# S4 convolution and gated FFN in one kernel: zero products moved behind the last z products, an `rs` operation and two groups of sums moved, z rooms filled by channel block

## The chip, the cores and the metric

The kernel runs on one core of a Trainium2 chip as one launch. The metric is device time in microseconds (us); the runs of a kernel are summed up by their median. The core's engines are PE (TensorE: matmuls, with PEld for the weight loads that overlap them), DVE (VectorE), ACT (ScalarE), POOL (GpSimd) and SP (SyncE, which only issues DMAs here). ACT and POOL issue DMAs too. Each engine works through its own instructions in order and waits by semaphores for the others.

## What is computed

The reference is an adaLN block on 2048 tokens of 640 channels, in float32. Cut to what matters:

```
h = layernorm(x) * (1 + ca) + sa
x = x + ga * s4(h)            # long convolution by FFT, plus u * Dskip
h = layernorm(x) * (1 + cb) + sb
gate, up = h @ w1, h @ w3     # 640 x 1728 each
x = x + gb * ((silu(gate) * up) @ w2)
```

`s4` builds a kernel of length 2048 for each channel from 128 complex modes and convolves it with `h`; the reference does it by FFT of twice the length.

## The kernel before

**First part, 0 to about 368 us.** The convolution is done as a two-step transform of 32 x 64 points, channel block by channel block (5 blocks of 128 channels). The result before its last step, called z, goes to a scratch in DRAM (`zs`) as it comes. The last step multiplies z by a constant matrix `i2` on PE.

**Second part, the output phase.** The tokens are 16 tiles of 128, in four quarters of four tiles; two quarters (A and B) make a pair. For each x tile, `x_get` (L1150 to 1162) loads the tile of x and its z rows, `x_mid` (L1164 to 1177) multiplies z by `i2` into PSUM, adds the result to x on DVE and takes the layer norm's statistics, `x_norm` normalises on ACT, and `x_turn` transposes four tiles at a time on PE into the operands `xA0` to `xA4` and `xB0` to `xB4`. The FFN has 14 blocks of 128 hidden channels, named f = 0 to 13; the last one is half as wide and has gate and up in one tile. All its matmuls are done in a split form: each operand is a high and a low part (`gh` and `gl` for the gate weights, `uh` and `ul` for the up weights, made by an ACT cast and a DVE subtraction), and each product is three matmuls. Blocks f = 0, 13, 1 and 2 of the first pair are done plainly (`plain`, L1280), quarter A first, then quarter B in the order 2, 1, 13, 0; the others go through `seven` (L1338), which does two quarters with seven block products in place of eight and needs sums of operands (`x_sums`, L1219, split by `x_sum_split`, L1229).

**The transition.** The tiles of quarter A are prepared in the first part, all but the last channel block, whose products (`late_products`, L811, into the bank `pls`) come last. `x_stats` (L832 to 845) adds them to x, takes statistics and aggregates them (BN_AGGR, one for each of four tiles) on DVE, has POOL compute the power -1/2 of the variance, and DVE form `rs[:, 2]`, the negative mean times that. Only ACT's normalisation reads `rs[:, 2]`; ACT normalises tiles 0 and 2, DVE tiles 1 and 3. `x_first` (L1138) begins with `keep_warm(18)`, 18 matmuls of zeros by zeros, 128 x 128 by 128 x 512, into a bank of the pool `psA`. Then come the 20 transposes. The tiles of quarter B (4 to 7) are prepared while PE works on f = 0, 13 and 1 of quarter A: `beside` (L1563) issues one of the steps in the list `side` (L1560) behind each group of products.

**The preparation of pair 1.** While PE does the `w2` products of pair 0 (`outputs`, L1398, 28 steps of 15 or 10 products), the function `prepare` (L1486) puts one step of preparing eight x tiles beside each step. Six of them have no room of their own for z: `homes` (L1497) lists two operand tiles of pair 0 for each, which are no longer read. z of an x tile is 128 partitions (64 frequencies for either part of the channel blocks: blocks 0 and 1 in partitions 0 to 63, blocks 2 to 4 in 64 to 127) by 4 row groups by 3 blocks of 128. With homes, each of the two tiles holds two of the four row groups, and `z_load` (L847) fills it with five DMAs of 64 x 2 x 128. SP issues all of these, in order with the loads of x and of `xs`. ACT issues the loads of `w2` (`load(n + 4, S)`, L1436) between its casts. `x_mid` does 8 products for each tile: four row groups by two halves, with 256 or 384 columns. A matmul in float32 is two instructions in the trace.

**What sets the order.** A scheduler orders the instructions by their place in the code, as resources come free; where `in_order` is set, and where `tc.keep_in_program_order` or `tc.issue_after` ask for it, the order written in the code holds. The two pools' banks and the number of buffers of each name make an instruction wait for the last reader of what it overwrites. Nearly all operations are issued through one helper, so the profile shows them under its line, L114, and tiles are told apart by name.

Of the kernel before, what the change touches and what calls it, by code (L numbers as in the profile page):

```python
# [17 lines left out]
P = 128  # L18
# [15 lines left out]
NG = NA // 8  # L34
NPG = NPH + NG - 1
LATE = 5
TURN = 4294967296.0
EPS = 1e-5

# [80 lines left out]
def tile_kernel(ctx: ExitStack, tc: tile.TileContext, a):  # L120
# [655 lines left out]
    def zj(k, j):  # L776
        return zs[k, j % 4, j // 4].rearrange("l c f d -> (c f) l d")
# [54 lines left out]
    def x_stats():  # L832

        mv = xp.tile([P, 4, 2], F32, name="mv4", bufs=1)
        rs = xp.tile([P, 3, 4], F32, name="rs4", bufs=1)
        for j, (x, z, st) in enumerate(early):
            V.tensor_tensor(x[:, 512:], pls[j][:, :P], x[:, 512:], op=OP.add)
            V.bn_stats(st[:, 4, :], x[:, 512:])
            V.bn_aggr(mv[:, j, :], st)
        e = lambda i: epst[:, i:i + 1].broadcast_to([P, 4])  # L840
        G.tensor_tensor(rs[:, 0, :], mv[:, :, 1], e(0), op=OP.add)
        power = G.tensor_tensor(rs[:, 1, :], rs[:, 0, :], e(1), op=OP.pow)
        V.scalar_tensor_tensor(rs[:, 2, :], mv[:, :, 0], -1.0, rs[:, 1, :], op0=OP.mult, op1=OP.mult)
        moments.extend((mv, rs))
        return power

    def z_load(z, j, ks, q=nc.sync, b0=0):  # L847

        nb = z.shape[1]
        for k in ks:  # L850
            hh = int(k > 1)
            kk = k - 2 * hh
            ins = q.dma_start(z[hh * 64:hh * 64 + 64, :, kk * DC:kk * DC + DC], zj(k, j)[:, b0:b0 + nb])
        return ins

    def x_tile():
# [194 lines left out]
    for tk in range(NS + 1, LAG + 8 * NDC + 2):  # L1051
        do("st", tk)
        do("kc", tk)
        if tk == LAG + 8 * NDC:
            late_products(6)
        last = do("iv", tk - 1)
        do("zt", tk - 1)
        do("T", tk)
        do("Y", tk)
        if tk == NS + 1:  # L1060
            tabs.close()
            xp = ctx.enter_context(tc.tile_pool(name="xp", bufs=2))
            idle = xp.tile([P, 512], F32R, name="idle", bufs=1)
            G.memset(idle.bitcast(F32), 0.0)
            for j in range(4):
                early[j] = (x_tile(), early[j][1], xp.tile([P, KD, 6], F32, name="st5", bufs=4))
                G.memset(early[j][1][64:, :, 2 * DC:], 0.0)
            i2bt = [h_tile() for _ in range(8 - LATE)]
        i = tk - 1 - LAG - 8 * NDC + 8
        if 0 <= i < 8:  # L1070
            if i < 4:
                z_last_load = z_load(early[i][1], i, (3,), q=nc.gpsimd)
            if i == 3:
                with tc.issue_after(z_last_load.ins):
                    for t in range(8 - LATE):
                        for j in range(4):
                            nc.gpsimd.dma_start(i2bt[t][j * 32:j * 32 + 8], a["i2b"][:, t])
            for j in ((), (), (), (), (0,), (1,), (), (2, 3))[i]:
                x_part(j, last)
            if i == 6:  # L1080
                pl = psS.tile([P, 2, 512], F32, name="pl", tag="A", bufs=1)
                pls += [pl[:, 0], pl[:, 1]] + [psS.tile([P, 512], F32, name="pl", tag=t, bufs=1) for t in ("pk", "pb")]
                late_products(5)
            if i == 7:
                z_early()
                early_products()
                late_products(7)
    power = x_stats()
    for name in first_w:
        first_w[name] = xp.tile([P, KD, P], F32, name="rw", bufs=4)  # L1090
# [25 lines left out]

        return wq.tile([P, 512], F32, name=f"s{i}")

    IDLE = 18

    def keep_warm(n):

        ps = bank(0)
        for _ in range(n):
            tc.keep_in_program_order(PE.matmul(ps, idle[:, :P], idle, start=True, stop=True))

    def pair_tile(name, dt=F32R):

        return wq.tile([P, 2, 512], dt, name=name)
# [7 lines left out]

    def x_first(tiles):  # L1138

        keep_warm(IDLE)  # L1140
        mv, rs = moments
        for j, (x, z, st) in enumerate(early):
            xn = xn_tile(j)
            if j % 2 == 0:
                S.activation(xn, x, AF.Identity, scale=rs[:, 1, j:j + 1], bias=rs[:, 2, j:j + 1])
            else:
                V.tensor_scalar(xn, x, mv[:, j, 0:1], rs[:, 1, j:j + 1], op0=OP.subtract, op1=OP.mult)
            tiles.append(xn)

    def x_get(j, x, loaded=False, homes=None):  # L1150

        if homes:
            zs_ = [pair_tile(n, F32).rearrange("p a b -> p (a b)")[:, :768].rearrange("p (b d) -> p b d", b=2)
                   for n in homes]
        else:
            zs_ = [z_tile()]
        with tc.issue_after(zlast[0].ins):
            if not loaded:
                SQ.dma_start(x, a["x"][j * P:(j + 1) * P, :])
            for i, z in enumerate(zs_):  # L1160
                z_load(z, j, range(NDC), SQ, 2 * i)
        return [x, [zs_[b * len(zs_) // 4][:, b % (4 // len(zs_))] for b in range(4)]]

    def x_mid(j, got, g):  # L1164

        x, z = got
        py = [bank(g) for _ in range(2)]
        for b in range(4):
            for hh in range(2):
                r, c = slice(hh * 64, hh * 64 + 64), slice(b * NA, b * NA + NA)  # L1170
                n = ZW[hh]
                PE.matmul(py[hh][c, :n], i2[r], z[b][r, :n], start=True, stop=True, tile_position=(r.start, c.start))
        for hh in range(2):
            h = slice(hh * 256, hh * 256 + ZW[hh])
            V.tensor_tensor(x[:, h], py[hh][:, :ZW[hh]], x[:, h], op=OP.add)
        got.extend(ln_stats(xp, x))
        G.dma_start(xs[j], x)
# [6 lines left out]
        tiles.append(xn)  # L1184

    ends = [None, None]

    def x_split(name, xf):
        t = pair_tile(name)
# [48 lines left out]
    def split(src, shape, names, after=None, part=slice(None)):  # L1238
        hi = wq.tile(shape, F32R, name=names[0], bufs=2)
        lo = wq.tile(shape, F32R, name=names[1], bufs=2)  # L1240
        with ExitStack() as order:
            for ins in after or ():
                order.enter_context(tc.issue_after(ins.ins))
            S.copy(hi[:, part], src[:, part])
            V.tensor_tensor(lo[:, part], src[:, part], hi[:, part].bitcast(F32), op=OP.subtract)
        return hi, lo

    def weight(f, name, q=None):
# [281 lines left out]
    for pair in range(2):  # L1530
# [37 lines left out]
        for n, f in enumerate(simple):  # L1568
# [6 lines left out]
            if pair == 0 and n == 1:  # L1575
                with tc.issue_after(power.ins):
                    for j, (x, z, st) in enumerate(early):
                        G.dma_start(xs[j], x)

        for n, f in enumerate(simple[::-1]):  # L1580
            hB[f] = h_tile()
            ws = ws or plain_weights(f)
            plain("B", f, hB[f], ws)
            ws = None
            if pair == 0 and n < 2:
                x_sums(n)
                x_sum_split(n)
        for i in range(2):
            x_late(i)
        before = output  # L1590
# [77 lines left out]
```

## Time and profile before

| | us |
|---|---|
| runs of before | 938.29, 936.25, 935.79 |
| median | 936.25 |
| the profiled execution's own time | 939.53 |
| its span, first to last instruction | 937.6 |
| what lies around the span | 1.93 |
| mean granted TensorE clock | 0.970 of full |

The profile is of one execution of its own, which took 3.28 us longer than the median of the runs. Its page lists busy time by engine and by group of instructions; the trace behind it has each instruction's start and length, the idle time before it and what ended that. Busy shares in slices of the span run from 0 to 9 tenths:

```profile
PE   4888879999998898999999999899999999999997
PEclk9977789999999998999999999999999999999999
```

Each digit is a fortieth of the span, 23.4 us. The output phase begins in the sixteenth slice.

### The profile page before, as it was taken

Reading aid. Unit: us, or ns where it says so; the run is one execution under the profiler, and the core shown is the slowest. Engines: PE = TensorE matmul, PEld = TensorE weight load, DVE = VectorE, ACT = ScalarE, POOL = GpSimd, SP = SyncE. Lnnn points to the kernel's source line nnn. Section 1 sums busy time; section 2 is a strip of 40 time slices with the busy share of each in tenths; the row PEclk is TensorE's granted clock in tenths of the full one; section 3 lists DMA queues with packets and bytes.
Section 4 is the critical chain, followed back from the end, with each engine's and each line's share of the span. In section 5 each row is a group of like instructions: output and inputs, shape, how many; then the busy total and the mean of one; then the engine's idle time right before and its main releaser. Section 6 shows DMA issues by size and latency. Waiting matters only on the chain.

```text
span 937.6 us, 20100 instructions
## 1 busy us (share of the span) xinstructions
PE 875.5 (93%) x8036; PEld 668.3 (71%) x8036; DVE 700.2 (75%) x1209; ACT 541.3 (58%) x747; POOL 272.7 (29%) x285
## 2 busy tenths in 40 slices
PE   4888879999998898999999999899999999999997
PEld 2545456666666576788888886578888888888786
DVE  5899889999999967685666665677976666654684
ACT  6988889999999542474333332475633333323332
POOL 3333434553454221223222202210332222200341
PEclk9977789999999998999999999999999999999999
DMA  9664375676566968942121227946311322123352
GB/s 270 217 222 175 133 211 179 212 192 192 171 210 191 299 202 227 290 149 75 56 57 57 57 82 213 260 148 195 101 57 56 113 57 57 56 87 97 98 187 93
DMA packets 103808, 140.68 MB, mean 150 GB/s; under 512 B 20420, under 2 KB 62916, under 8 KB 103716
## 3 DMA queue, kind: packets, MB, share of 16 engines
q1 hardware_dynamic: 93012, 113.71, 40.2%
q10 hardware_dynamic: 8272, 18.16, 6.4%
q0 software_dynamic: 2432, 7.54, 2.5%
q8 instruction: 63, 1.03, 0.5%
q14 instruction: 29, 0.24, 0.1%
HBM read 107.92 MB, written 31.46 MB: 149 GB/s over the span
## 4 chain that ended last, share of the span: by engine, by line
PE 74%; ACT 9%; DVE 8%; issue 3%; SPq 3%; DMA 3%; DVEq 0%; ACTq 0%
PE ps L114 54%; PE p L114 7%; PE pz L114 4%; PE pt L114 3%; SPq L114 3%; PE pk L114 2%; PE pa L114 2%; ACT A L114 2%; ACT cs L114 1%; DVE uk L114 1%; DVE u L114 1%; ACT ph L114 1%; PE pu L114 1%; ACT uk L114 1%; ACT L114 1%
## 5 line engine op out<-in xcount | busy, mean ns | idle before, releaser
L114 DVE TENSOR_TENSOR s<-ps,s 128x512 f32<-128x512 f32 x138 | 94.9, 687 | 82.5 <-PE ps L114 82.2
L114 ACT CAST gh<-rw 128x640 fp32r<-128x640 f32 x87 | 63.3, 728 | 128.3 <-PE ps L114 86.4
L114 DVE TENSOR_TENSOR gl<-rw,gh 128x640 fp32r<-128x640 f32 x87 | 78.0, 896 | 69.0 <-ACT gh L114 68.6
L114 POOL TENSOR_TENSOR S<-rw 128x256 f32<-128x256 f32 x46 | 36.9, 805 | 234.9 <-DVE S0l L114 157.4
L114 PE MATMUL ps<-gh,uh 128*128 128x512 f32 x224 | 88.1, 393 | 0.0
L114 PE MATMUL ps<-gl,uh 128*128 128x512 f32 x224 | 87.7, 392 | 0.0
L114 PE MATMUL ps<-xA,gh 128*128 128x512 f32 x280 | 87.6, 391 | 0.0
L114 PE MATMUL p<-uk,s 128*64 128x256 f32 x576 | 71.6, 391 | 15.2 <-DVE Y L114 3.9
L114 POOL TENSOR_TENSOR ph<-thi,iota 128x1376 int32<-128x1376 int32 x20 | 51.2, 2562 | 117.8 <-DVE A L114 103.6
L114 DVE TENSOR_TENSOR E<-A,cs 128x1024 f32<-128x1024 f32 (+1 forms) x80 | 80.6, 1019 | 1.9 <-PE pk L114 1.3
L114 PE MATMUL ps<-gh,ul 128*128 128x512 f32 x208 | 81.6, 392 | 0.0
L114 ACT ACTIVATE A<-pa 128x1024 f32<-128x1024 f32 (+1 forms) x80 | 64.4, 815 | 10.2 <-PE pa L114 9.8
L114 PEld LDWEIGHTS p<-uk,s 128*64 128x64 f32 x576 | 41.3, 138 | 36.9 <-DVE Y L114 5.6
L114 PEld LDWEIGHTS ps<-xA,gh 128*128 128x128 f32 x280 | 52.3, 188 | 12.5 <-ACT xA L114 0.7
L114 DVE TENSOR_TENSOR A<-A,ph 128x1024 f32<-128x1024 f32 x40 | 54.1, 1357 | 0.8
L114 PE MATMUL ps<-xA,gl 128*128 128x512 f32 x140 | 54.5, 389 | 0.0
L114 PE MATMUL pt<-s,K 128*64 128x128 f32 x640 | 45.1, 284 | 6.1 <-ACT uk L114 5.9
L114 PEld LDWEIGHTS ps<-gl,uh 128*128 128x128 f32 x224 | 42.5, 190 | 9.1
L114 PEld LDWEIGHTS ps<-gh,uh 128*128 128x128 f32 x224 | 42.5, 190 | 9.0 <-DVE h L114 0.2
L114 ACT ACTIVATE s<-ps 128x512 f32<-128x512 f32 (+1 forms) x33 | 19.7, 597 | 45.8 <-PE ps L114 45.8
L114 POOL TENSOR_TENSOR rw<-rw,gbr 128x512 f32<-128x512 f32 x14 | 20.4, 1458 | 88.7 <-DMA rw<-in_w_dram 77.3
L114 PEld LDWEIGHTS pt<-s,K 128*64 128x64 f32 x640 | 35.6, 140 | 14.5 <-ACT uk L114 9.7
(224 smaller groups left out, 2227.2 us busy)
## 6 DMA issues: line engine op xcount, KB each, us to landing
rw<-in_w_dram ACTq DMA_DIRECT2D x44, 320.0 KB, 3.0
us<-u SPq DMA_DIRECT2D x16, 640.0 KB, 3.5
rw<-in_wg_dram SPq DMA_DIRECT2D x31, 320.0 KB, 3.0
s<-in_s_dram SPq DMA_DIRECT2D x36, 256.0 KB, 4.0
i<-in_i_dram SPq DMA_DIRECT2D x36, 256.0 KB, 4.7
rw<-in_wu_dram SPq DMA_DIRECT2D x28, 320.0 KB, 2.9
uk<-us SPq DMA_DIRECT2D x16, 512.0 KB, 5.6
zs<-zt SPq DMA_DIRECT2D x16, 512.0 KB, 4.7
```

Source lines behind the costliest of these rows:

```text
L114: ins = fn(*args, **kw)
```

## The change

Four places change.

1. The zero products move from the head of `x_first` to right behind `late_products(7)`, ahead of `x_stats`. They are 16 now, and they go into the PSUM bank with the tag "Z", which the first part used for z.
2. `rs[:, 2]` moves from `x_stats` to `x_first` and is issued behind the last subtraction of the weight split of f = 0 (`last_split`). That split waits for `last_sum`, which is now the last BN_AGGR.
3. `x_get` with homes puts two channel blocks of all four row groups into the first tile ("wide") and one into the second ("narrow"). z comes in five DMAs of 64 x 4 x 128 for each x tile in place of ten of 64 x 2 x 128, and `x_mid` does 12 products with 256, 256 and 128 columns in place of 8 with 256 and 384.
4. `x_sums(n)` and `x_sum_split(n)` of the first two plain blocks of quarter B are issued behind `ends[1]`, the last DVE operation of the last `x_turn`.

```diff
--- before.py
+++ after.py
@@ -34,6 +34,7 @@
 NG = NA // 8
 NPG = NPH + NG - 1
 LATE = 5
+IDLE = 16
 TURN = 4294967296.0
 EPS = 1e-5
 
@@ -836,21 +837,19 @@
         for j, (x, z, st) in enumerate(early):
             V.tensor_tensor(x[:, 512:], pls[j][:, :P], x[:, 512:], op=OP.add)
             V.bn_stats(st[:, 4, :], x[:, 512:])
-            V.bn_aggr(mv[:, j, :], st)
+            last_sum[0] = V.bn_aggr(mv[:, j, :], st)
         e = lambda i: epst[:, i:i + 1].broadcast_to([P, 4])
         G.tensor_tensor(rs[:, 0, :], mv[:, :, 1], e(0), op=OP.add)
         power = G.tensor_tensor(rs[:, 1, :], rs[:, 0, :], e(1), op=OP.pow)
-        V.scalar_tensor_tensor(rs[:, 2, :], mv[:, :, 0], -1.0, rs[:, 1, :], op0=OP.mult, op1=OP.mult)
         moments.extend((mv, rs))
         return power
 
-    def z_load(z, j, ks, q=nc.sync, b0=0):
-
-        nb = z.shape[1]
+    def z_load(z, j, ks, q=nc.sync):
+
         for k in ks:
             hh = int(k > 1)
             kk = k - 2 * hh
-            ins = q.dma_start(z[hh * 64:hh * 64 + 64, :, kk * DC:kk * DC + DC], zj(k, j)[:, b0:b0 + nb])
+            ins = q.dma_start(z[hh * 64:hh * 64 + 64, :, kk * DC:kk * DC + DC], zj(k, j))
         return ins
 
     def x_tile():
@@ -1085,6 +1084,9 @@
                 z_early()
                 early_products()
                 late_products(7)
+    ps = psS.tile([P, 2, 512], F32, name="ps", tag="Z", bufs=1)[:, 0]
+    for _ in range(IDLE):
+        tc.keep_in_program_order(PE.matmul(ps, idle[:, :P], idle, start=True, stop=True))
     power = x_stats()
     for name in first_w:
         first_w[name] = xp.tile([P, KD, P], F32, name="rw", bufs=4)
@@ -1116,14 +1118,6 @@
 
         return wq.tile([P, 512], F32, name=f"s{i}")
 
-    IDLE = 18
-
-    def keep_warm(n):
-
-        ps = bank(0)
-        for _ in range(n):
-            tc.keep_in_program_order(PE.matmul(ps, idle[:, :P], idle, start=True, stop=True))
-
     def pair_tile(name, dt=F32R):
 
         return wq.tile([P, 2, 512], dt, name=name)
@@ -1137,8 +1131,9 @@
 
     def x_first(tiles):
 
-        keep_warm(IDLE)
         mv, rs = moments
+        with tc.issue_after(last_split[0].ins):
+            V.scalar_tensor_tensor(rs[:, 2, :], mv[:, :, 0], -1.0, rs[:, 1, :], op0=OP.mult, op1=OP.mult)
         for j, (x, z, st) in enumerate(early):
             xn = xn_tile(j)
             if j % 2 == 0:
@@ -1150,16 +1145,22 @@
     def x_get(j, x, loaded=False, homes=None):
 
         if homes:
-            zs_ = [pair_tile(n, F32).rearrange("p a b -> p (a b)")[:, :768].rearrange("p (b d) -> p b d", b=2)
-                   for n in homes]
+            wide, narrow = (pair_tile(n, F32).rearrange("p a b -> p (a b)") for n in homes)
+            wide = wide.rearrange("p (k b d) -> p k b d", k=2, b=4)
+            z = [wide[:, 0], wide[:, 1], narrow[:, :4 * DC].rearrange("p (b d) -> p b d", b=4)]
+            use = [(0, 2 * DC, wide.rearrange("p k b d -> p b k d")), (2 * DC, 3 * DC, z[2])]
         else:
-            zs_ = [z_tile()]
+            t = z_tile()
+            z = [t[:, :, k * DC:k * DC + DC] for k in range(3)]
+            use = [(0, 3 * DC, t)]
         with tc.issue_after(zlast[0].ins):
             if not loaded:
                 SQ.dma_start(x, a["x"][j * P:(j + 1) * P, :])
-            for i, z in enumerate(zs_):
-                z_load(z, j, range(NDC), SQ, 2 * i)
-        return [x, [zs_[b * len(zs_) // 4][:, b % (4 // len(zs_))] for b in range(4)]]
+            for k in range(NDC):
+                hh = int(k > 1)
+                r = slice(hh * 64, hh * 64 + 64)
+                SQ.dma_start(z[k - 2 * hh][r], zj(k, j))
+        return [x, use]
 
     def x_mid(j, got, g):
 
@@ -1168,8 +1169,12 @@
         for b in range(4):
             for hh in range(2):
                 r, c = slice(hh * 64, hh * 64 + 64), slice(b * NA, b * NA + NA)
-                n = ZW[hh]
-                PE.matmul(py[hh][c, :n], i2[r], z[b][r, :n], start=True, stop=True, tile_position=(r.start, c.start))
+                for lo, hi, part in z:
+                    n = min(hi, ZW[hh]) - lo
+                    if n > 0:
+                        rhs = part[r, b] if len(part.shape) == 4 else part[r, b, :n]
+                        PE.matmul(py[hh][c, lo:lo + n], i2[r], rhs, start=True, stop=True,
+                                  tile_position=(r.start, c.start))
         for hh in range(2):
             h = slice(hh * 256, hh * 256 + ZW[hh])
             V.tensor_tensor(x[:, h], py[hh][:, :ZW[hh]], x[:, h], op=OP.add)
@@ -1184,6 +1189,7 @@
         tiles.append(xn)
 
     ends = [None, None]
+    last_split = [None]
 
     def x_split(name, xf):
         t = pair_tile(name)
@@ -1242,7 +1248,7 @@
             for ins in after or ():
                 order.enter_context(tc.issue_after(ins.ins))
             S.copy(hi[:, part], src[:, part])
-            V.tensor_tensor(lo[:, part], src[:, part], hi[:, part].bitcast(F32), op=OP.subtract)
+            last_split[0] = V.tensor_tensor(lo[:, part], src[:, part], hi[:, part].bitcast(F32), op=OP.subtract)
         return hi, lo
 
     def weight(f, name, q=None):
@@ -1577,14 +1583,16 @@
                     for j, (x, z, st) in enumerate(early):
                         G.dma_start(xs[j], x)
 
+        turned = ends[1]
         for n, f in enumerate(simple[::-1]):
             hB[f] = h_tile()
             ws = ws or plain_weights(f)
             plain("B", f, hB[f], ws)
             ws = None
             if pair == 0 and n < 2:
-                x_sums(n)
-                x_sum_split(n)
+                with tc.issue_after(turned.ins):
+                    x_sums(n)
+                    x_sum_split(n)
         for i in range(2):
             x_late(i)
         before = output
```

The order on the engines moves as follows. In the rows, a name with a number is one tile among several of its name, and x4 counts equal instructions in a row.

DVE, end of the first part, before: BN_AGGR is the aggregate, `gl` and `ul` are the low parts of f = 0's weights, the row with `rs_4831` on both sides is `rs[:, 2]`, and the TENSOR_SCALAR rows normalise tiles 1 and 3.

```order
L114 BN_STATS st_4431<-xm 128x6
L114 BN_AGGR mv_4830<-st_4428 128x2
L114 TENSOR_TENSOR gl<-rw,gh 128x640
L114 BN_AGGR mv_4830<-st_4431 128x2
L114 TENSOR_TENSOR ul<-rw,uh 128x640
L114 SCALAR_TENSOR_TENSOR rs_4831<-mv_4830,rs_4831 128x4
L114 TENSOR_SCALAR T_4897<-xm,mv_4830,rs_4831 128x640
L114 TENSOR_SCALAR T_4901<-xm,mv_4830,rs_4831 128x640
```

The same place now:

```order
L115 BN_STATS st_4431<-xm 128x6
L115 BN_AGGR mv_4847<-st_4428 128x2
L115 BN_AGGR mv_4847<-st_4431 128x2
L115 TENSOR_TENSOR gl<-rw,gh 128x640
L115 TENSOR_TENSOR ul<-rw,uh 128x640
L115 SCALAR_TENSOR_TENSOR rs_4848<-mv_4847,rs_4848 128x4
L115 TENSOR_SCALAR T_4895<-xm,mv_4847,rs_4848 128x640
L115 TENSOR_SCALAR T_4899<-xm,mv_4847,rs_4848 128x640
```

The fourth aggregate has moved in front of `gl`.

ACT, around the `s` of f = 0 (s_5020), before. The first `uh` is the up weight of f = 1 and the first `gh` its gate weight; the `s` of f = 13 has 64 rows, T_5046, T_5095 and T_5120 are the normalised tiles 4 to 6, s_5192 is the `s` of f = 1, and the `gh` behind the 64-row `s` is the gate weight of f = 2:

```order
L114 CAST uh<-rw 128x640
L114 ACT_TABLE_LOAD
L114 ACTIVATE s_5020<-ps 128x512
L114 CAST gh<-rw 128x640
L114 ACTIVATE T_5046<-xm,rs 128x640
L114 ACTIVATE s_5069<-ps 64x512
L114 CAST gh<-rw 128x640
L114 ACTIVATE T_5095<-xm,rs 128x640
L114 ACTIVATE T_5120<-T_4971,rs 128x640
L114 ACTIVATE s_5192<-ps 128x512
L114 CAST uh<-rw 128x640
```

The same place now (s_5018 for f = 0, T_5044, T_5093 and T_5118 for tiles 4 to 6, s_5190 for f = 1):

```order
L115 ACT_TABLE_LOAD
L115 ACTIVATE s_5018<-ps 128x512
L115 CAST gh<-rw 128x640
L115 CAST uh<-rw 128x640
L115 ACTIVATE s_5067<-ps 64x512
L115 ACTIVATE T_5044<-xm,rs 128x640
L115 ACTIVATE T_5093<-xm,rs 128x640
L115 ACTIVATE T_5118<-T_4969,rs 128x640
L115 ACTIVATE s_5190<-ps 128x512
L115 CAST gh<-rw 128x640
L115 CAST uh<-rw 128x640
```

The cast of f = 2's gate weight has moved behind the norms of tiles 4 to 6 and the `s` of f = 1; the cast of f = 1's up weight, which stood ahead of the table load, stands behind f = 1's gate weight.

SP, the z transfers of pair 1's first homed tiles, before:

```order
L114 DMA xA_6646<-zs 64x2x128 x5
L114 DMA xA_6647<-zs 64x2x128 x5
L114 DMA xA_6658<-zs 64x2x128 x5
L114 DMA xA_6659<-zs 64x2x128 x5
L114 DMA xA_6695<-zs 64x2x128 x5
```

And now:

```order
L115 DMA xA_6644<-zs 64x4x128 x4
L115 DMA xA_6645<-zs 64x4x128
L115 DMA xA_6651<-zs 64x4x128 x4
L115 DMA xA_6652<-zs 64x4x128
L115 DMA xA_6683<-zs 64x4x128 x4
```

Each x tile has five transfers of 64 x 4 x 128 (four into the wide tile, one into the narrow one) in place of ten; SP's order around them is as before.

On PE, the 20 transposes behind the zero products stand in another order, so that the ninth completes the first operand, and the products of two x_mids of quarter B (tiles 6 and 7) lie in two groups each, with products of f = 1 between them.

## The prediction

> **What bounds the kernel now.** I read the page's busy times first, then the granted clocks by stretches, then each engine's timeline around the places that the change touches.
>
> ```profile
> span 937.6 us, 20100 instructions
> PE 875.5 (93%) x8036; PEld 668.3 (71%) x8036; DVE 700.2 (75%) x1209; ACT 541.3 (58%) x747; POOL 272.7 (29%) x285
> ...
> 366.53:369.94 3.41, 2.43 (x80) 1.94 (x64) 2.99 (x14) 0.00 (x0) 0.00 (x0) 1.00 0.96 318
> 369.94:373.35 3.41, 2.65 (x6) 2.15 (x7) 2.90 (x10) 1.35 (x2) 0.64 (x1) 0.50 0.99 200
> 480.00:560.00 80.00, 80.00 (x354) 66.28 (x353) 52.02 (x89) 28.83 (x55) 13.76 (x19) 1.00 0.21 61
> 575.00:584.98 9.98, 9.98 (x65) 6.48 (x64) 6.26 (x14) 2.19 (x4) 4.22 (x12) 1.00 0.90 272
> 584.98:588.39 3.41, 2.25 (x10) 1.46 (x8) 1.03 (x2) 1.78 (x3) 0.76 (x2) 1.00 0.67 184
> 591.81:595.22 3.41, 1.98 (x21) 0.62 (x19) 1.43 (x2) 2.07 (x3) 0.97 (x3) 1.00 1.16 212
> 595.22:598.63 3.41, 3.41 (x8) 2.71 (x9) 1.26 (x2) 2.02 (x3) 0.00 (x0) 0.50 1.10 327
> ```
>
> A row of the stretches has its length, then busy time and count of PE, PEld, DVE, ACT and POOL, then the granted clock, the DMA share and GB/s. PE works in 93% of the span. In the products of the first pair (480 to 560 us) it never idles and has full clock: there only less matrix work would help, and the change removes none. What can be won lies in two holes, the transition into the output phase (369 to 387 us) and the preparation of pair 1's x tiles (565 to 603 us). In both PE idles, and at 369.94 and 595.22 the clock falls to a half; a stretch of 3.41 us at half costs 3.41 x 0.5 = 1.71 us of work.
>
> **Transition: the zero products and the moved `rs` operation.**
>
> ```profile
> 367.79 1.17 PE L114 MATMUL pl<-zt,h 8*128 8x128 f32 x32
> 370.70 7.19 PE L114 MATMUL ps<-idle 128*128 128x512 f32 x18 [1.73 <-DVE xm L114]
> 377.72 2.35 PE L114 MATMUL ps<-ident,T 128*128 128x128 f32 x20
> 387.20 0.88 PE L114 MATMUL ps<-A,i 64*32 64x256 f32 x16
> 370.86 0.27 DVE L114 BATCH_NORM_AGGREGATE mv<-st 128x2 f32<-128x30 f32 x1
> 371.57 0.83 DVE L114 TENSOR_TENSOR gl<-rw,gh 128x640 fp32r<-128x640 f32 x1 [0.44 <-DMA A<-zs]
> 372.31 0.28 DVE L114 BATCH_NORM_AGGREGATE mv<-st 128x2 f32<-128x30 f32 x1
> 373.40 1.04 POOL L114 TENSOR_TENSOR rs<-rs,epst 128x4 f32<-128x4 f32 x1
> 374.67 1.74 ACT L114 ACTIVATE T<-xm,rs 128x640 f32<-128x640 f32 x2 [2.51 <-DVE rs L114]
> 378.36 0.78 ACT L114 ACTIVATE xA<-ps,modT 128x512 fp32r<-128x512 f32 x1 [1.95 <-PE ps L114]
> ```
>
> A timeline row has start and length, and in brackets the idle time before it with what ended it. The last z products end at 367.79 + 1.17 = 368.96. PE idles 1.73 us, as the zero products take a bank whose sums DVE still reads (`xm`). The 18 zero products fill 370.70 to 377.72, while the last normalised tile is there at 374.67 + 1.74 = 376.41: the transposes wait 1.3 us for products that compute nothing. Now 16 start at 368.96. The 354 instructions of 480 to 560 us stand 80.00 / 354 = 0.226 us apart, so at full clock the 16 end at 368.96 + 3.6 = 372.6; at half clock, twice that, at 376.2.
>
> The tiles come earlier too. The fourth aggregate stands behind `gl`, which waits for ACT. The third started at 370.86, so in front of `gl` the fourth starts near 371.05, not 372.31: 1.25 us. POOL's two operations follow (the second ends at 374.44 now), so the power ends near 373.2 and the last tile near 375.2. The moved `rs` operation stands behind `ul` (the old `gl` at 371.57 with 0.83, and a second split like it: 373.1), hence in POOL's shadow: the move costs nothing while POOL ends later than `ul`. Without that cover it costs the overhang, some tenths.
>
> At full clock the transposes go at 374.4, when the first two tiles are there, the first `xA` near 375.5 instead of 378.36, and f = 0 ends (387.20) 2.9 earlier. At half clock the transposes start at 376.2 instead of 377.72, 1.5 earlier, the last of them perhaps slower too: 1.3. Which it is hangs on PE's activity. The stretch 366.53 to 369.94, with PE busy 2.43 of 3.41 us in small products, was followed by half clock; the change fills its last microsecond with wide ones, and opens a gap of at most 1.8 us (372.6 to 374.4) behind them instead. I take **-2.3**, nearer the full-clock end, with ends -2.9 and -1.3. [...]
>
> **What f = 2 meets.** ACT's cast of f = 2's gate weight, before right behind the `s` of f = 13, now stands behind the norms of tiles 4 to 6 and the `s` of f = 1.
>
> ```profile
> 393.78 0.71 ACT L114 CAST gh<-rw 128x640 fp32r<-128x640 f32 x1
> 400.41 0.93 ACT L114 ACTIVATE T<-xm,rs 128x640 f32<-128x640 f32 x1 [5.91 <-POOL rs L114]
> 401.24 0.91 ACT L114 ACTIVATE T<-T,rs 128x640 f32<-128x640 f32 x1
> 402.05 0.58 ACT L114 ACTIVATE s<-ps 128x512 f32<-128x512 f32 x1
> 397.92 0.80 DVE L114 TENSOR_TENSOR gl<-rw,gh 128x640 fp32r<-128x640 f32 x1
> 401.07 0.62 PE L114 MATMUL ps<-xA,gh 128*128 128x512 f32 x2
> ...
> 413.47 0.50 PE L114 MATMUL ps<-xB,gh 128*128 128x512 f32 x1 [0.40 <-DVE xB L114]
> ```
>
> The cast ran at 393.78 and PE wanted it at 401.07, 13.9 behind the end of f = 0. Behind the `s` it would start at 402.05 + 0.5 by the old times and be there at 403.2, 16.0 behind that end. The norms gain, since DVE's splits (0.8 each) leave the places between its statistics: some 1.2 us, so +14.7 for the cast and 0.8 more for `gl`, which PE wants one product pair (0.46) later. PE stalls 0.8 to 1.1. Queued behind the cast are f = 2's other casts and the norm of tile 7, with microseconds to spare. Also, two x_mids now lie in two groups among products, at one or two more switches of shape each (0.1 to 0.3). Together **+1.5**; the ends are 0 (the norms gain twice as much) and +3 (they gain nothing).
>
> The x_sums behind the last turn: at 413.47 PE waits for an `xB` that stands behind x_sums on DVE. The 0.40 goes, and the 0.11 by which that product is longer than the 0.39 of its neighbours: **-0.5**. Late next are the x_sums' splits, used much later; ends -0.6 and +0.5 (one split of DVE, 0.8, hit in part).
>
> **Preparing pair 1: z by channel block.**
>
> ```profile
> 573.67 7.31 SPq L114 DMA_DIRECT2D T<-zs  x10
> 588.82 3.75 SPq L114 DMA_DIRECT2D A<-zs  x5
> 586.17 0.33 ACTq L114 DMA_DIRECT2D rw<-in_w_dram  x1
> 586.61 0.72 ACT L114 CAST gh<-rw 128x640 fp32r<-128x640 f32 x1 [5.12 <-DMA T<-zs]
> 567.38 0.88 PE L114 MATMUL ps<-xA,i 64*32 64x256 f32 x16
> 571.82 1.67 PE L114 MATMUL ps<-xA,i 64*32 64x256 f32 x16
> 581.50 1.58 PE L114 MATMUL ps<-xB,i 64*32 64x256 f32 x16
> 587.90 0.50 PE L114 MATMUL ps<-uh,gh 128*128 128x512 f32 x1 [1.16 <-ACT uh L114]
> 594.21 0.51 PE L114 MATMUL ps<-uh,gh 128*128 128x512 f32 x1 [1.32 <-ACT uh L114]
> ```
>
> SP issues ten 64x2x128 transfers in 7.31 us and five 64x4x128 (the A rooms) in 3.75: 0.73 and 0.75 each, whatever their size. The six tiles with homes go from 60 issues to 30, some 44 us of SP's queue to 22. This matters because ACT's own weight load waits for such a transfer: the load of `w2` issues at 586.17 and the cast at 586.61 had idled 5.12 us for a `T<-zs`. Behind the late cast PE idles 1.16 and 1.32 us, each with a slow first product (0.50 for 0.39), then again for the low half: the idle part of the two stretches is 3.41 - 2.25 = 1.16 and 3.41 - 1.98 = 1.43. The half clock from 595.22 costs 1.71. Two x_mids take 1.67 and 1.58 instead of 0.88, as DVE adds behind the late splits: 1.49. Together 1.16 + 1.43 + 1.71 + 1.49, and some 0.5 for the slow products: 6.3. If SP runs ahead, ACT's load no longer meets an open transfer, and all of it goes. Against it: an x_mid of a homed tile has 24 instructions for 16 at the same columns; an instruction costs nothing more if the columns set the time, and 0.88 / 16 = 0.05 if each does, 0.4 for eight, so 0 to 2.4 for six tiles. I take 0.6, nearer to the columns' end, since 256 columns stream through in 0.1 us at the product's rate of 512 in 0.226, above the 0.05 of a short instruction. **-5.7**; ends -6.8 (other small stalls too) and 0 (the waits stay).
>
> **Sum.** -2.3 + 1.5 - 0.5 - 5.7 = -7.0 us against the profiled execution's 939.53 (span 937.6 and 1.93 around it): 932.5. That execution is 3.28 above the median of the runs, 936.25. Its half clocks may be among what the others lack, and then the gain there is not had either. If all of -7.0 holds for the median, it comes to 929.2, if none of the 3.28 does, to 932.5; I take the middle, **930.9**.
>
> **Rivals.**
> - *The prep waits stay (0.20).* The DMA share is 0.90 at 272 GB/s in 575 to 585 us and above 1.1 at 595: if the rings, not SP's issues, set when z lands, half as many issues of twice the size land as late. For it: those shares; against it: SP issues 0.7 us apart without a pause, as an issue-bound queue does. Then only -2.3 + 1.5 - 0.5 = -1.3 is had: 935.0 from the median.
> - *The cast of f = 2 stalls PE for long (0.08).* If the norms gain nothing and the gap also takes a half-clock stretch: +3 and 1.71, so -2.3 + 4.7 - 0.5 - 5.7 = -3.8: 932.5 to 935.7.
> - *Denser z traffic delays the weights (0.06), slower.* SP's 64 KB per 0.73 us is 90 GB/s, 128 KB per 0.75 is 175. With what else moves (272 - 90 = 180) that asks for 355 GB/s, more than the 327 of the best row here. If ACT's loads pay, each of some six casts between 570 and 600 us is late by as much as the two now seen, 1.3 us and up, plus half clock: +6.3 in place of -5.7, 936.25 - 1.3 + 6.3 = 941.3. It decides from the point at which a load lands later than one tile's products last, 571.82 - 567.38 = 4.4 us.
> - *The transition gives nothing (0.06).* The norms, not the zero products, set the start, and half clock stays: 0 for -2.3, 933.2.
>
> **How the numbers follow.** The forecast has 0.60. About 0.3% (2.8 us) is what a measurement of this kernel can tell from no change, so faster is below 933.4, slower above 939.1. The forecast is nearly all faster (0.57), the second and last rival about half (0.07), the first a third (0.07): 0.71, with slower 0.06 and 0.23 between. Low end: -2.9 + 0 - 0.6 - 6.8 = -10.3 on 939.53 and 3.28 off is 926.0; high end: the first rival at 935.0, with f = 2 at its worse end 936.5. I cut the outer half microsecond of both: 926.5 to 936.0.
>
> **What would show it.** Right: zero products from 369 with no idle time before them; the first `xA` 2 to 3 us earlier; PE waiting under 2 us for f = 2's `gh`; no wait at x_sums; SP's z issues over by about 580; no `DMA` wait above 3 us ahead of ACT's casts in 575 to 600; full clock at 595. Wrong: half clock behind the zero products, a long wait ahead of f = 2, or ACT's casts still released by z transfers.

## The result, and the profile after

| | before | changed |
|---|---|---|
| median of six runs each, us | 937.75 | 930.93 |
| lowest and highest | 935.79, 939.50 | 930.14, 937.06 |
| ratio of the changed to before, 95% interval | | 0.9948 (0.9929 to 0.9967) |
| the profiled execution and its span | 939.53, 937.6 | 937.06, 935.1 |

The change makes the kernel faster by 0.5%. The six runs of before include the three that were shown; three more were taken beside the changed kernel. A second set of runs of the changed kernel (below) has a median of 930.01 and a ratio of 0.9922 (0.9904 to 0.9941).

The profiled execution of the changed kernel is the slowest of its six, so it is read here place by place and not as a whole. First the transition, in the timelines of PE, DVE, POOL and ACT (start, length, instruction, idle time before it and what ended that):

```profile
368.46 1.17 PE L115 MATMUL pl<-zt,h 8*128 8x128 f32 x32
369.56 3.92 PE L115 MATMUL ps<-idle 128*128 128x512 f32 x16
375.07 2.45 PE L115 MATMUL ps<-ident,T 128*128 128x128 f32 x20 [1.58 <-ACT T L115]
385.18 0.88 PE L115 MATMUL ps<-A,i 64*32 64x256 f32 x16
371.53 0.42 DVE L115 BATCH_NORM_AGGREGATE mv<-st 128x2 f32<-128x30 f32 x2
372.31 1.55 POOL L115 TENSOR_TENSOR rs<-rs,epst 128x4 f32<-128x4 f32 x1
374.09 1.73 ACT L115 ACTIVATE T<-xm,rs 128x640 f32<-128x640 f32 x2 [1.36 <-DVE rs L115]
```

The zero products follow the z products without a gap and run at full clock (granted 1.00), 16 in 3.92 us. The two last aggregates run together, and what PE waits for is now the normalised tile (`ACT T`), 1.58 us. From the end of the z products to the end of f = 0 it takes 385.18 - (368.46 + 1.17) = 15.55 us; before, 18.23.

The next stretch, up to f = 2, in PE's and ACT's timelines:

```profile
389.63 1.09 PE L115 MATMUL ps<-A,i 64*32 64x256 f32 x24
391.77 0.85 PE L115 MATMUL ps<-A,i 64*32 64x384 f32 x8
395.27 0.64 PE L115 MATMUL ps<-A,i 64*32 64x256 f32 x8
397.42 0.85 PE L115 MATMUL ps<-A,i 64*32 64x384 f32 x8
400.37 0.62 PE L115 MATMUL ps<-xA,gh 128*128 128x512 f32 x2
398.28 0.57 ACT L115 ACTIVATE s<-ps 128x512 f32<-128x512 f32 x1
398.75 0.71 ACT L115 CAST gh<-rw 128x640 fp32r<-128x640 f32 x1
```

f = 2 starts 400.37 - 385.18 = 15.19 us behind f = 0, where it was 13.87. PE has no idle time ahead of it (no bracket), although the cast of its weights (398.75) now stands behind the norms. What has grown is PE's own row of products: the x_mids of tiles 6 and 7 are cut into groups of one half of z each.

The preparation of pair 1 in this execution, ACT's casts, one pair of DVE's additions and PE, and the stretches around them (length, then busy time and count of PE, PEld, DVE, ACT, POOL, then granted clock, DMA share, GB/s):

```profile
587.01 0.72 ACT L115 CAST gh<-rw 128x640 fp32r<-128x640 f32 x1 [5.44 <-DMA xm<-in_x_dram]
593.06 0.72 ACT L115 CAST gh<-rw 128x640 fp32r<-128x640 f32 x1 [3.98 <-DMA rw<-in_w_dram]
595.16 0.88 DVE L115 TENSOR_TENSOR xm<-ps,xm 128x256 f32<-128x256 f32 x2
588.31 0.50 PE L115 MATMUL ps<-uh,gh 128*128 128x512 f32 x1 [0.16 <-ACT uh L115]
595.64 1.31 PE L115 MATMUL ps<-T,i 64*32 64x256 f32 x22 [2.60 <-DVE xm L115]
...
592.59:596.00 3.41, 0.81 (x16) 0.32 (x18) 2.18 (x4) 2.94 (x5) 0.00 (x0) 1.00 1.10 214
596.00:599.41 3.41, 3.41 (x30) 2.61 (x16) 3.26 (x8) 1.70 (x3) 1.74 (x4) 0.50 0.91 310
```

No z transfer stands in the brackets any more, but ACT's load still waits for another transfer once, for 5.44 us. That wait costs PE only 0.16 us (588.31). ACT idles 3.98 us more ahead of the next cast, at 593.06, until a load of weights has landed. DVE's additions to x, whose banks PE waits for, come at 595.16, behind the split that follows that cast; PE idles 2.60 us, and half clock follows (0.50 from 596.00 to 599.41). So this execution lost about 5 us of what the change saves.

### The profile page after: what moved, and what is told of

Read it like the earlier page. It is cut to its first block, busy times and chain, and to the rows that moved or that the text cites. A ratio compares the mean times of both kernels' runs of the same rounds, so it can differ in the third digit from the quotient of the medians.

```text
span 935.1 us, 20139 instructions
## 1 busy us (share of the span) xinstructions
PE 873.9 (93%) x8082; PEld 668.0 (71%) x8082; DVE 700.7 (75%) x1209; ACT 542.0 (58%) x747; POOL 273.8 (29%) x285
## 4 chain that ended last, share of the span: by engine, by line
PE 73%; DVE 9%; ACT 8%; DMA 5%; issue 3%; POOL 0%; SPq 0%; DVEq 0%; ACTq 0%; POOLq 0%
PE ps L115 54%; PE p L115 6%; PE pz L115 3%; PE pt L115 2%; PE pk L115 2%; DMA rw<-in_w_dram 2%; PE pa L115 2%; PE pu L115 2%; ACT A L115 1%; DVE A L115 1%; DVE uk L115 1%; DVE E L115 1%; ACT cs L115 1%; DVE u L115 1%; ACT uk L115 1%
```

## The experiments

All traces give the same four stretches of PE's timeline, from one execution each. The table lists them in us: from the end of the z products (zero products excluded) to the end of f = 0, taken as the start of the x_mid behind it; from there to quarter B's first product; from there to the first `w2` product; from there to the end of the last matmul. The median and the ratio stand beside them.

| kernel | z to f = 0 | to quarter B | to `w2` | to the end | median | ratio (95% interval) |
|---|---|---|---|---|---|---|
| before | 18.23 | 22.83 | 147.06 | 375.65 | | |
| changed, first profile | 15.55 | 24.14 | 146.42 | 374.67 | 930.93 | 0.9948 (0.9929, 0.9967) |
| after_again | 17.18 | 24.15 | 146.41 | 369.60 | 930.01 | 0.9922 (0.9904, 0.9941) |
| rooms_only | 18.09 | 22.87 | 147.09 | 370.27 | 932.15 | 0.9953 (0.9934, 0.9973) |
| no_rooms | 15.54 | 24.14 | 146.41 | 375.71 | 934.69 | 0.9973 (0.9961, 0.9986) |
| rooms_ten | 15.56 | 24.14 | 146.41 | 376.03 | 937.26 | 1.0001 (0.9982, 1.0021) |
| zeros_only | 16.42 | 24.14 | 146.64 | 374.39 | 937.98 | 1.0004 (0.9988, 1.0019) |
| sums_only | 17.56 | 22.83 | 147.11 | 373.40 | 937.12 | 1.0003 (0.9984, 1.0021) |
| whole_mids | 15.51 | 25.05 | 146.46 | 369.77 | 932.22 | 0.9946 (0.9926, 0.9966) |
| one_group | 15.52 | 24.75 | 146.47 | 369.97 | 929.55 | 0.9917 (0.9895, 0.9940) |
| early_split | 15.75 | 25.10 | 146.43 | 369.07 | 930.90 | 0.9933 (0.9916, 0.9950) |
| kept_all | 15.51 | 22.89 | 146.45 | 370.05 | 930.18 | 0.9934 (0.9908, 0.9960) |
| no_zeros | 17.04 | 26.94 | 146.45 | 369.01 | 936.51 | 0.9996 (0.9978, 1.0014) |
| zeros24 | 15.99 | 32.64 | 146.45 | 369.75 | 937.47 | 1.0002 (0.9985, 1.0018) |

The ratios go against before on the same chip. The first part, up to the z products, ends between 365.85 and 370.86 us in these executions, whatever the kernel; that scatter is in every time and in none of the four columns.

**after_again**: the changed kernel once more, no edit.

> The changed kernel once more, for a second profiled execution beside the first (937.06 us, which idled 2.60 us at 595.64 and had half clock from 596.00 to 599.41). Theory A (the z transfers' ring waits and the half clock behind them are chance, they fall in some executions): time near 930 to 931, and if this execution is one of those, no idle time of PE above 1 us between 565 and 605 us and no half clock there. Rival B (they come in every execution): the same idle time near 595 as in the first profile, and what differs between 930 and 937 lies in another place.

PE is busy throughout the 50 us from the first `w2` product, at full clock. The first row is before, the second the changed kernel's first profile, the third this one:

```profile
557.09:607.09 50.00, 47.31 (x276) 32.30 (x275) 29.15 (x56) 18.60 (x30) 11.87 (x29) 0.97 0.85 232
555.74:605.74 50.00, 47.13 (x330) 35.00 (x329) 30.33 (x59) 19.26 (x30) 13.10 (x30) 0.97 0.98 238
553.74:603.74 50.00, 50.00 (x370) 37.60 (x369) 33.92 (x66) 23.49 (x37) 15.46 (x35) 1.00 0.97 245
```

Theory A holds: PE's waits fall in some executions of the changed kernel only. The DMA engines are busier than before (0.97 against 0.85) and PE loses nothing, so here a high DMA share alone did not hold PE; how many transfers were queued behind it, the profile doesn't say. The same wait still stands on ACT, and misses PE:

```profile
583.67 0.73 ACT L115 CAST gh<-rw 128x640 fp32r<-128x640 f32 x1 [4.10 <-DMA xm<-in_x_dram]
```

It comes 583.67 - 553.74 = 29.93 us behind the first `w2` product; in the first profile it came at 587.01 - 555.74 = 31.27. That 1.3 us is not what separates nothing from 5 us: in one_group (below) this cast comes later still, 584.24 - 552.59 = 31.65 us behind, and PE loses 0.54 us. The cast after it differs: 586.76 here, 33.0 us behind the first `w2` product, 586.45 in one_group (33.9), 593.06 in the first profile (37.3).

**rooms_only and no_rooms**: the z rooms alone on before (the lines of `x_get` below and those of `x_mid`); and the changed kernel with these lines as before.

```diff
-            zs_ = [pair_tile(n, F32).rearrange("p a b -> p (a b)")[:, :768].rearrange("p (b d) -> p b d", b=2)
-                   for n in homes]
+            wide, narrow = (pair_tile(n, F32).rearrange("p a b -> p (a b)") for n in homes)
+            wide = wide.rearrange("p (k b d) -> p k b d", k=2, b=4)
...
+                SQ.dma_start(z[k - 2 * hh][r], zj(k, j))
```

> The kernel before with the z rooms of the output phase filled by channel block, nothing else. Theory A (prediction: this part carries -5.7 of -7.0): 932 to 933 against 937.75 of before. Rival B (the waits of the preparation stay, the gain is from the transition): within 1 us of before. By the profile of the changed kernel, whose preparation still idled, something between, 934 to 936, would say that the waits go in part.

> The changed kernel with the z rooms, their transfers and x_mid as before: the transition and the x_sums alone. Theory A: -2.3 of the transition, +1.3 for the two cut x_mids as the changed kernel's profile shows them, -0.5 of the x_sums: 936 to 936.5 against 937.75. Rival B: 932 to 933, the whole gain.

The rooms alone give 932.15 where before on the same chip has 936.63, -4.5, and the rest alone -1.9 by the medians (-2.5 by the ratio); the two parts add up to about the whole on that chip (936.63 - 930.01 = 6.6). In the table the rooms act on the last column alone, 375.65 to 370.27.

**rooms_ten**: the new rooms with ten issues.

```diff
-                SQ.dma_start(z[k - 2 * hh][r], zj(k, j))
+                for i in range(2) if homes else (None,):
+                    rows = slice(None) if i is None else slice(2 * i, 2 * i + 2)
+                    SQ.dma_start(z[k - 2 * hh][r, rows], zj(k, j)[:, rows])
```

> The changed kernel with each of the five z transfers of a homed tile issued as two of 64x2x128: the same rooms, the same 12 products, the same bytes, 60 issues again. Theory A (the number of issues on SP sets how late z lands and thereby ACT's weight loads): the preparation idles again as in before, 5 to 6 us of PE between 565 and 605 us, time 935 to 936. Rival C (the layout of the rooms or the order of the blocks is what helps, not the issues): 930 to 931 as the changed kernel.

Same rooms, products and bytes, twice the issues of half the size: the whole gain of the last column is gone (376.03). So the number of issues carries it, and not the layout of the rooms. By the four columns rooms_ten should still be 1.6 us faster than before, and 935 to 936 was expected; its median is no faster, and the interval, which reaches 1.7 us below before, only just allows for that. SP's queue (start, length, transfers) of rooms_ten first, then of after_again:

```profile
565.39 7.95 SPq L115 DMA_DIRECT2D xB<-zs  x12
574.08 7.55 SPq L115 DMA_DIRECT2D T<-zs  x10
582.30 7.26 SPq L115 DMA_DIRECT2D T<-zs  x10
...
542.37 14.11 SPq L115 DMA_DIRECT2D xA<-zs  x14
561.99 4.97 SPq L115 DMA_DIRECT2D T<-zs  x5
569.78 3.81 SPq L115 DMA_DIRECT2D T<-zs  x5
```

In rooms_ten the second `T` group is issued until 589.56, 32.6 us behind the first `w2` product (556.97); in after_again until 573.59, 19.9 us behind it, and there are pauses in the queue. Whether it is SP's time alone, or also that twice as many transfers stand between ACT's load and the one it has to wait for, was not told apart. Each larger transfer took SP longer: the homed rooms (`xA`, `xB` and `T`) have 40.9 us for 60 issues in before, and 28.9 and 27.4 us for 30 in the changed kernel's two profiles.

**zeros_only and sums_only**: the zero products alone (moved, 16); the fourth aggregate and the `rs` operation alone. Both are pieces of the change's diff put into before.

> The kernel before with the zero products moved and cut to 16, nothing else. Theory A: the end of the z products to the end of f = 0, 18.24 us in before and 15.55 in the changed kernel, becomes 16.5 to 17 at full clock, as the normalised tiles (fourth aggregate behind gl) set the start; the cut x_mids cost 1.32 behind it, so the time is within 1 us of before. Rival: the whole 2.7 is had without the moved sums.

> The kernel before with the fourth aggregate in front of gl and the rs operation behind the weight split, nothing else. Theory A: the tiles are ready 1.2 us earlier and wait for the 18 zero products, so the end of the z products to the end of f = 0 stays at 18.0 to 18.3 and the time with it. Rival: the stretch falls by 1 us or more.

Neither changes the median. zeros_only shortens the first column from 18.23 to 16.42 and lengthens the second by 1.31, since the scheduler cuts the x_mids as soon as the zero products have moved. sums_only has 17.56, as its tiles wait for 18 zero products; the 0.67 under before is what those took less (6.52 us for 7.19). Only together do they reach 15.55: the first frees PE, the second brings what PE then waits for. In no_rooms, which has both, they are worth the 2.7.

**whole_mids, one_group, early_split, kept_all**: the cut x_mids. whole_mids keeps the products of x_mid in the order of the code (first piece, in all four kernels). one_group and early_split also begin with the other half of z (second piece). early_split and kept_all split f = 2's weights in the code ahead of those x_mids and order the norms of tiles 5 and 6 behind the cast (third piece). kept_all begins with the same half as before, takes the first product of each plain block of quarter A into the kept order, and orders the casts of quarter B's f = 1 behind tile 7's norm (fourth piece).

```diff
+                        if not g:
+                            tc.keep_in_program_order(ins)
...
-            for hh in range(2):
+            for hh in ((0, 1) if g else (1, 0)):
...
+                later = {i: plain_weights(i) for i in simple[2:]}
+                cast2 = casts[-2]
+                with tc.issue_after(cast2.ins) if i in (1, 2) else ExitStack():
+                    x_norm(4 + i, got[i], tiles)
...
+                if hold and i + j == 0:
+                    tc.keep_in_program_order(ins)
+            ws = ws or plain_weights(f, [norm7] if pair == 0 and n == 1 else None)
```

> The changed kernel with the products of the transition's x_mids kept in the order of the code, so that the two halves of z alternate nearly throughout (one product, then seven in a row) in place of four of one half and four of the other. Theory A (products of the two halves run side by side when they alternate, and the 1.32 us by which f = 0's end to f = 2's start grew, 13.87 to 15.19, is their being cut): 14.0 to 14.3 for that stretch and about 1 us less in time. Rival B (ACT's cast of f = 2 behind the norms sets that start): 14.7 or more, with PE idle for gh or gl, and under 0.5 us less in time.

> The changed kernel with the x_mids of the transition in the order of the code and beginning with the other half of z, so that PE meets each x_mid in one piece (three cuts of the row of products for the tiles 5 to 7, where the changed kernel has four groups and before had two). Theory D (each group of z products between other products costs about half a microsecond beside its columns, since a group of one product took 0.54 and one of seven 0.80): f = 0's end to f = 2's start falls from 15.19 to 14.4 to 14.7, time 0.5 to 0.8 us less. Rival B (ACT's cast of f = 2 sets the start once PE is faster): PE idles ahead of f = 2 and the stretch stays at 15.

> The x_mids in one piece as in one_group, and ACT's cast of f = 2's gate weight ahead of the norms of tiles 5 and 6 by an added order. Theory D with the cast as second limit: f = 0's end to f = 2's start, 15.19 in the changed kernel and 15.50 in one_group (1.09 of it PE waiting for gh), falls to 14.3 to 14.6, with no idle time of PE there; time 0.6 to 0.9 us under the changed kernel, about 929.5 to 930. Rival: the norms, later now, hold the transposes of quarter B, and PE idles there instead by 1 us.

> The changed kernel with quarter B's x_mids in one piece as before (their products and the first products of f = 1 kept in the order of the code), ACT's cast of f = 2 ahead of the norms of tiles 5 and 6, and the norm of tile 7 ahead of quarter B's next weight casts. Theory D (the 1.32 us between f = 0's end and f = 2's start are the two cuts, and nothing else is late once the cast and the norm have their old places): f = 0's end to f = 2's start 13.8 to 14.1 (15.19 in the changed kernel), f = 0's end to quarter B's first product 22.8 to 23.3 (24.14), and about 1 us less in time, 929 to 930. Rival: as in early_split the norm of tile 7 comes late through DVE and POOL, the second stretch stays at 24 or more, and so does the time.

whole_mids: PE, the cut x_mid of tile 7 and the rest of it, then what waits behind:

```profile
392.79 0.62 PE L115 MATMUL ps<-A,i 64*32 64x256 f32 x2
393.33 0.73 PE L115 MATMUL ps<-xA,uh 128*128 128x512 f32 x2
394.92 0.87 PE L115 MATMUL ps<-A,i 64*32 64x384 f32 x14
395.72 0.72 PE L115 MATMUL ps<-xA,uh 128*128 128x512 f32 x2
402.48 1.20 PE L115 MATMUL ps<-ident,T 128*128 128x128 f32 x9 [0.68 <-ACT T L115]
```

One product of z between others holds PE 0.54 us (392.79 to 393.33), the seven left 0.80, as much as all eight in one piece. In the changed kernel four and four hold it 0.56 and 0.78 (395.27 to 395.83, 397.42 to 398.20). f = 2 starts 397.90 - 382.71 = 15.19 behind f = 0's end, as in the changed kernel. So the expectation of 14.0 to 14.3 failed: how the halves alternate doesn't matter, the cut itself costs half a microsecond. With the cuts gone the forecast wait appears. one_group, then kept_all:

```profile
396.87 0.73 PE L115 MATMUL ps<-xA,gh 128*128 128x512 f32 x2 [1.09 <-ACT gh L115]
...
393.74 0.72 ACT L115 CAST gh<-rw 128x640 fp32r<-128x640 f32 x1
397.56 0.62 PE L115 MATMUL ps<-xA,gh 128*128 128x512 f32 x2
```

In one_group PE idles 1.09 us for f = 2's cast. In early_split the cast is early, and PE idles 1.68 us for tile 7's norm in the transposes of quarter B instead (second column 25.10). kept_all has all three in place: f = 2 starts 397.56 - 383.62 = 13.94 behind f = 0's end (13.87 before), and the column is 22.89. That is 1.25 us less than in the changed kernel, but the medians (930.18 against 930.93 and 930.01, from three sets of runs) don't resolve it.

**no_zeros and zeros24**: `IDLE = 0` and `IDLE = 24` in the changed kernel.

> The changed kernel without the zero products (0 for 16). Theory A: PE idles some 5.4 us from the last z products to the transposes, the clock falls to a half in one or two stretches of 3.41 us and costs 1.7 to 3.4; but the scheduler orders the x_mids of quarter B as in before, in one piece, 1.3 less: time 0.4 to 2 us over the changed kernel. Rival E (the zero products are not needed, the transposes and the first products raise the clock within a stretch): 1 us or more under the changed kernel.

> The changed kernel with 24 zero products for 16, which at full clock end 5.5 us behind the last z products, as the first tile comes. Theory A: the tiles set the start, so the end of the z products to the end of f = 0 stays near 15.5 to 15.9 at full clock, and the gap in which the second profile of the changed kernel lost its clock (373.2 to 376.6) is filled: time as the changed kernel within 1 us. Rival: the zero products run late and hold the transposes, 1 us or more.

Without zero products PE idles 6.22 us, and half clock reaches from 367.9 to 378.1 (10.2 us, granted 0.50 to 0.51); the first profile, with 16, has 1.00 from 367.31 to 380.96. The first column is 17.04, 1.5 more than with 16. Both kernels also lose in the second column. In no_zeros PE waits 3.89 us for a norm in the transposes of quarter B, whose cause was not followed up. In zeros24 the scheduler's order is another: a load of an x tile for pair 1 now stands on SP ahead of quarter B's z:

```profile
362.76 2.36 SPq L1099 DMA_DIRECT2D xm<-in_x_dram  x2
374.18 0.33 SPq L1621 DMA_DIRECT2D xm<-in_x_dram  x1
374.68 3.54 SPq L115 DMA_DIRECT2D A<-zs  x5
394.42 0.64 PE L115 MATMUL ps<-A,i 64*32 64x256 f32 x8 [2.02 <-DMA A<-zs]
```

The load goes at 374.18, over 9 us behind the one before it, and quarter B's first z group starts 374.68 - 367.87 = 6.8 us behind the end of the z products; in the changed kernel's first profile it starts at 367.91, 1.7 us ahead of it. PE then waits for z (2.02 us here) and for weights. So these two times don't price zero products; the first column does.

## Why the prediction was right

930.9 was forecast for the median and 930.93 measured. So close a hit is luck: from the 936.25 that was known the forecast took off 5.35 us, while the six runs of before have 937.75 and the change took off 6.82. Both differences are about 1.5 us and cancel. The terms are what counts.

- **Preparing pair 1, forecast -5.7.** Right in cause: with half the issues PE stops waiting. The size was a little too large. The five kernels with 60 issues need 373.40 to 376.03 in the last column, mean 375.0; eight of the nine profiles with 30 need 369.01 to 370.27, mean 369.7, the ninth 374.67. That is -5.3 between these means, -4.8 with the ninth, and -4.5 by the median of rooms_only.
- **Steps of that term that were wrong.** "0.73 and 0.75 each, whatever their size": 14 transfers of the first group took 14.11 us, 1.0 each, and SP's queue fell by 12 to 14 us, not from 44 to 22. It did no harm, as they are early. "ACT's load no longer meets an open transfer": it still does, and the sign "no `DMA` wait above 3 us" failed in both profiles (5.44, 4.10). What changed is how often. In before five casts between 561 and 587 us idle 2.79 to 5.12 us for a z transfer; in after_again one idles 4.10 us for an x transfer and one 1.02 us for z. The 12 products of an x_mid took 0.03 us more than 8 (0.83 for 0.80), 0.2 for six tiles where 0.6 was taken.
- **Rivals of that term.** A loss as large as in "the waits stay" came in one of nine executions, behind loads of x and weights and not of z. As the rival of denser traffic had it, z lands later (the `T` rooms, median from issue to landing: 4.1 us before, 7.7 and 6.7 in the two profiles), but eight of nine last columns show no cost of it.
- **Transition, forecast -2.3 between -2.9 and -1.3.** 15.55 for 18.23 is -2.7, the full-clock case. Seven of the eight other profiles with both parts and 16 or 24 zero products lie at 15.51 to 15.99. The one exception is after_again, at 17.18 (-1.05). It is the gap behind the zero products that was feared: the tiles came later there (a gap of 2.46 us for 1.58), and the clock fell to 0.50 from 373.22 to 376.63. The place of the `rs` operation has a part in it. The weight split of f = 0 came late, since ACT's cast (first row) idled until a transfer of z to `zs` was done. POOL's power was ready at 368.68 + 1.04 = 369.72, but `rs[:, 2]`, which the code now orders behind the split (on DVE it stood behind `ul` in before as well), started at 371.16. So the overhang without POOL's cover, put at "some tenths", was 1.4 us here, and the tiles came that much later. In the first profile POOL ended at 373.86 and `rs[:, 2]` started at 373.90: there it cost nothing, as forecast.

```profile
368.92 0.73 ACT L115 CAST gh<-rw 128x640 fp32r<-128x640 f32 x1 [6.43 <-DMA zs<-zt]
368.68 1.04 POOL L115 TENSOR_TENSOR rs<-rs,epst 128x4 f32<-128x4 f32 x1
370.42 0.82 DVE L115 TENSOR_TENSOR ul<-rw,uh 128x640 fp32r<-128x640 f32 x1
371.16 0.16 DVE L115 SCALAR_TENSOR_TENSOR rs<-mv,rs 128x4 f32<-128x4 f32 x1
372.32 3.83 PE L115 MATMUL ps<-ident,T 128*128 128x128 f32 x20 [2.46 <-ACT T L115]
369.81:373.22 3.41, 0.95 (x9) 0.84 (x9) 2.55 (x5) 2.20 (x3) 2.15 (x4) 1.00 0.94 232
373.22:376.63 3.41, 3.41 (x16) 3.31 (x16) 1.94 (x3) 2.79 (x5) 0.00 (x0) 0.50 1.03 360
```

- **f = 2, forecast +1.5.** The size was right (+1.32) and the step was wrong. "PE stalls 0.8 to 1.1" for the cast did not happen in the changed kernel; the cut x_mids, put at "0.1 to 0.3" a switch, took the whole 1.32, 0.66 a cut, and hid the cast, which was there at 399.46 - 385.18 = 14.28 (forecast 14.7; 16.0 less 1.2 is 14.8). The stall itself was well reckoned: it is there at 1.09 once the cuts are gone (one_group).
- **x_sums, forecast -0.5.** The third column falls by 0.64. zeros_only, which leaves the x_sums in their place, has 0.42 of it; so only some 0.2 is shown for the moved x_sums themselves.
- **Median against profile.** Half of the 3.28 was taken off as a middle, with no row behind it. By the columns the changed kernel saves 2.7 + 5.3 + 0.6 - 1.3 = 7.3 us in a typical execution, and the two ratios say 4.9 and 7.3.

## What to carry to other kernels

A queue that only issues can set the pace of another engine, as SP's 60 issues did here (last column 376.03 us with 60, 369.60 and 374.67 with 30): count the issues and look for pauses, and try fewer, larger transfers before looking at bytes. Two waits that end near each other have to go together for the whole gain: the zero products alone took 1.8 of the 2.7 us off the first column, the sums alone 0.7, and that by shorter zero products. An operation placed behind work that may come late needs more cover than one profile shows (1.4 us in after_again, nothing in the first profile). A few instructions moved in a scheduled kernel can reorder what stands 20 us later: compare the orders there, and price a cut between unlike products by the trace (0.66 us each here).

## What was unexpected

The clock fell to a half after a stretch in which PE was busy 0.95 of 3.41 us (after_again, 369.81 to 373.22; granted 0.50 in the next), and not behind the gap of 1.58 us in the first profile, which lies across two stretches with PE busy 2.77 and 2.48 of 3.41 us (370.72 to 377.55; granted 1.00 there and in the next). Busy time alone doesn't decide it: 2.43 of 3.41 us in small products was followed by half clock in before, and 2.49 in no_zeros (364.46 to 367.87). What else has a part in it, these runs do not show. A lone product of z between the FFN's products held PE 0.54 us and four of 256 columns 0.56: three more were nearly free once the cut was paid. Four of 384 columns held it 0.78, as much as all eight of both halves (0.80).
